# Two first blocks of expert 0 cut at different batches, with operand tiles of their own, and score banks handed over after the last scores

## The chip, the cores and the metric

The kernel runs on one core of a Trainium2 chip. A core has five engines that each work through their own instructions in order: TensorE (PE, matrix products; PEld is its weight load), VectorE (DVE), ScalarE (ACT), GpSimd (POOL) and SyncE (SP), which issues most DMA transfers. GpSimd issues the gathers and scatters by row number. Products land in PSUM, eight banks of 128 partitions by 512 fp32. The metric is the device time of one execution in microseconds (us).

## The reference

Windowed attention for 8 batches, 8 heads, 576 positions and 64 columns per head, followed by a mixture of experts over the 4608 token rows of 512 columns:

```
scores = q k^T / 8 - slope * distance, kept where 0 <= i - j < 128
attn   = softmax(scores);  x = attn v            (rows: batch, position)
noisy  = x w_gate + log(1 + exp(x w_noise)) * noise
the two best of 8 experts per row, their weights by softmax over the two
out[row] = sum over the two: weight * relu(x[row] w1[e]) w2[e]      (512 -> 1024 -> 512)
```

## The kernel before

The kernel is written out by a planner. Each piece of work is a Python generator ("strand") that asks for engines, tiles and events; `Order` keeps a simulated time, a queue by rank for every engine (lower ranks first) and rings of free tiles, and emits an instruction when the simulated engine is free. So the order on each engine is fixed when the program is built, by ranks and by constants in the head of the file (STAGE, LATE, GATE and so on), and the hardware then runs each engine's list in order. A rank is roughly a place in attention: pair k of heads and block i have 5k + i, and attention ends at 160.

**Attention.** 32 pairs of heads (4 per batch) are each cut into three units of one or two blocks of 128 queries. For a unit `unit` takes two score banks from the ring `sb` (two sets of two banks), TensorE computes scores (L493, L486), VectorE adds the bias and writes them to SBUF (`top`, L509 to L519), and gives the banks back. ScalarE takes exponentials (L526), TensorE transposes them (L533), GpSimd masks the window (L553, L554), TensorE multiplies with the values into an output bank of `ob` (L574). When the four pairs of a group are done, `row_major` turns the output into token rows: TensorE transposes, VectorE divides into a tile x (L678, a ring of four), SyncE stores it (L683) to `xs` in DRAM.

**Routing.** `gate` and `route(b)` compute the gate of a batch, choose two experts per row, count rows per expert in `base` and write every row's number into the slot lists of its experts in DRAM (a scatter on GpSimd, L900). Routing goes from batch to batch, since the counts carry over.

**Experts.** Each expert's list is worked off in blocks. `tokens` gathers a block's rows from `xs` (GpSimd, L1147), `fit` scales each row by a power of two and splits it into two fp16 parts (VectorE L1168 to L1172, ScalarE for the upper part), and a DMA transpose puts them into the operand tiles xh and xl. `ups` multiplies with a chunk of w1 into a hidden bank from `hbr` (L1200, twelve products for 128 hidden columns), `middle` takes the positive part and splits it (L1220, L1235) into hh and hl, `downs` multiplies with w2 into output banks from `yb` (L1244), and `result` scales, and scatters to `out` with an add (L1333).

**The first two blocks.** The first 768 rows of expert 0 are worked on before the lists are complete. After the routing of batch 6 (`CUT`), `base` of expert 0 is raised to at least 768 (L777), so no later row falls below, and the list's first 768 row numbers are read (`fetch_ids`, L940) and clipped to the rows of six batches (L920). Both blocks, 384 rows each, become known then. They share one pair of operand tiles xh and xl, so the second block's gathers wait until the first block's last `ups` has read them (L1228). Ranks of the two blocks go from FFN0 to FFN1, behind attention; their gathers and fits come TOKENS ranks ahead.

**Banks.** `hbr` and `yb` are empty during attention. `banks` waits until all units are done (`attended`), and hands three score banks to `hbr` and one to `yb`, then the two output banks to `yb`.

**The second wave.** When attention and routing are over, their pool of tiles is closed, a second pair of operand tiles, more weight sets and buffers are opened in its place, and the rest of expert 0 (448 rows, called the third block here) and the seven other experts follow, all on the same TensorE queue. Their weights are split to two fp16 parts on the way (L1136 for the lower part).

Of the kernel before, what the change touches and what calls it, by code (L numbers as in the profile page):

```python
# [8 lines left out]
F32 = mybir.dt.float32  # L9
F16 = mybir.dt.float16  # L10
# [11 lines left out]
NQ = 5  # L22
# [4 lines left out]
FIRST = ((0, 384), (384, 384))  # L27
FROWS = sum(c for _, c in FIRST)
# [12 lines left out]
LOAD = -26.0  # L41
VALUES = -0.5
GATE = (-11.1, 63.1)
ROUTE = 6.1
SCATTER = (9.2, -1042.6, -37.6)
FFN0, FFN1 = 178.3, 232.3
WEIGHTS = (79.4, 86.4)
TOKENS = 85.5
STAGE = (-3.5, 10.2, 17.3, -7.2, 18.8, 24.7, 17.7, -20.9)
MIDDLE = 41.7  # L50
RESULT = -82.8
# [3 lines left out]
LATE = (-6.5, -33.9, 75.9, 86.5, 26.5, -92.0, 67.3, -71.1, 43.6, -25.4, 8.5, -25.7)  # L55
# [4 lines left out]
SWITCH, NEAR = 0.093, 6.4  # L60
# [152 lines left out]
class Block:  # L213


    def __init__(self, e, s0, n, rows, rings):
        self.e, self.s0, self.n, self.rows, self.rings = e, s0, n, rows, rings
        self.last = self.flip = False
        self.tiles = [(j, min(128, n - 128 * j)) for j in range((n + 127) // 128)]
        self.ready, self.ids, self.back, self.left = Event(len(self.tiles)), Event(), Event(), len(self.tiles)  # L220
        self.weighed = Event(len(self.tiles))
        self.h = [(Event(), []) for _ in range(8)]
# [3 lines left out]
def attention_moe(ctx: ExitStack, tc: tile.TileContext, qk_, v, w_gate, w_noise, noise, w1, w2,  # L226
# [56 lines left out]
    xr = ring(ap_, 4, [128, DM], F32, "x")  # L283
# [36 lines left out]
    least = const.tile([128, 1, E], F32, name="least")  # L320
# [51 lines left out]
    def set_ups():  # L372
# [21 lines left out]
        def columns():  # L394
            reached = tmp[0:E * SPAN, 0]
            nc.vector.tensor_scalar(reached, mine, 0.0, None, op0=OP.is_ge)
            nc.vector.tensor_reduce(tmp[0:E * SPAN, 1, 0:1], reached[:, 1:E], axis=AX.X, op=OP.add)
            nc.vector.scalar_tensor_tensor(first_line, tmp[0:E * SPAN, 1, 0:1], float(LINES - SPAN), first_line,
                                           op0=OP.mult, op1=OP.add)
            nc.vector.scalar_tensor_tensor(mine, mine, float(SPAN), reached, op0=OP.is_lt, op1=OP.mult)  # L400
            nc.vector.tensor_copy(line_of[0], first_line)
            nc.vector.tensor_scalar(least[:, 0], iota8, float(NF), float(FROWS), op0=OP.is_lt, op1=OP.mult)
# [173 lines left out]
    over, attended = Event(n + B + B * NQ), Event(n)  # L576
# [10 lines left out]
    def unit(u):  # L587
# [8 lines left out]
        s = yield (sb, r0)  # L596
        yield pe((0.77, 0.98, 0.325)[gr], r0, lambda: scores(k, blocks, s), mode="rows" if nz == 2 else "full")
# [147 lines left out]
    def route(b):  # L745
# [29 lines left out]
        def up():  # L775
            if b + 1 == CUT:
                V.tensor_tensor(base, base, least[:, 0], op=OP.max)  # L777
# [131 lines left out]
        if b + 1 == CUT:  # L909
            for j in range(FROWS // 128):  # L910
                spawn(fetch_ids(j, rank))
            yield fetched
            for z in range(CUT):
                yield stored[z]

            def clipped():
                for s0, c in FIRST:
                    z = slice(s0 // 128, (s0 + c) // 128)
                    tokens_of(lists[:, z, 0], ix.bitcast(F32)[:, z], spare[:, 0:c // 128])
                nc.vector.tensor_scalar(cl, ix, float(CUT * S - 1), None, op0=OP.min)  # L920

            yield dve(0.4, rank, clipped)
            for blk in first:
                blk.ix, blk.at = (v[:, blk.s0 // 128:(blk.s0 + blk.n) // 128] for v in (ix, cl))
                mark(blk.ids)
                spawn(weights_back(blk, rank))
# [12 lines left out]
    def fetch_ids(j, rank):  # L939
        yield from move(1e4, rank, lambda: nc.sync.dma_start(lists[:, j], dram(slots, j * 128, [[1, 128], [1, 1]])))  # L940
        mark(fetched)
# [7 lines left out]
    fetched = Event(FROWS // 128)  # L949
# [21 lines left out]
    rings = {r: Ring([block_tiles(keep, r, z) for z in range(c)]) for r, c in (("xh", 1), ("xl", 1), ("hh", 3), ("hl", 3))}  # L971
    ixr, ytr = Ring([]), Ring([])
    first = [Block(0, s0, c, CUT * S, rings) for s0, c in FIRST]
# [166 lines left out]
    def tokens(blk, rank):  # L1140
        yield blk.ids
        blk.gw = yield (gwr, rank)
        blk.xh = yield (rings["xh"], rank)
        blk.xl = yield (rings["xl"], rank)
        for j, r in blk.tiles:
            xg = yield (xgr, rank)
            yield pool(1.04, rank, lambda: nc.gpsimd.indirect_dma_start(  # L1147
                out=xg[0:r], out_offset=None, in_=xs[0:blk.rows],
                in_offset=bass.IndirectOffsetOnAxis(ap=blk.at[0:r, j:j + 1], axis=0)))
            spawn(turn_tokens(blk, j, r, xg, rank))  # L1150
# [73 lines left out]
    def middle(blk, f, t, rank, end):  # L1224
        c = blk.n
        yield end
        if f == 7:
            put(rings["xh"], blk.xh)  # L1228
            put(rings["xl"], blk.xl)
# [125 lines left out]
    def banks():  # L1355

        yield attended
        scores_ = [t for two in (sb.free.pop(), sb.free.pop()) for t in two]
        for t in scores_[:3]:
            put(hbr, t)  # L1360
        put(yb, scores_[3])
# [4 lines left out]
    def second_wave():  # L1366
# [3 lines left out]
        for r in ("xh", "xl"):  # L1370
            put(rings[r], block_tiles(more, r, 1))
# [238 lines left out]
```

## Time and profile before

| what | value |
|---|---|
| median of 3 runs | 1079.54 us (1079.49 to 1082.17) |
| the profiled execution | 1074.51 us |
| its span, first to last instruction | 1072.7 us |
| busy: TensorE, VectorE, ScalarE, GpSimd | 1022.9, 703.0, 448.0, 360.1 us |
| mean granted TensorE clock | 0.991 of full speed |
| moved by DMA | 178.62 MB |

The span is that of one profiled execution; its own time is 1.8 us longer. Busy time counts an instruction from start to end, and products overlap, so a busy TensorE can still wait for short times. In a timeline row stand the start, the duration, the engine, the line, the operation, the tiles (written <- read), and in brackets the idle time before it with what ended it. A granted clock of 1.0 is 2.4 GHz, 0.5 is 1.2 GHz.

### The profile page before, as it was taken

How to read it: one execution, taken by the hardware profiler on the slowest of the kernel's cores; microseconds unless marked ns; L12 is line 12 of the kernel's file. 1: busy time of each engine (PE TensorE's matmuls, PEld its weight loads, DVE VectorE, ACT ScalarE, POOL GpSimd, SP SyncE). 2: the span in 40 equal slices, each digit the busy share in tenths (PEclk: the TensorE clock that was granted, in tenths of full speed). 3: DMA queues.
4: the chain of work that ended last, by engine and by line, in shares of the span. 5: the costliest groups of instructions: out<-in, count | busy, mean ns of one | idle time of the engine just before them, and what ended most of it. 6: DMA issues, size and time to landing. Idle time of an engine off the chain costs nothing. (4 is left out here: it accounts for less than half of the span.)

```text
span 1072.7 us, 20464 instructions
## 1 busy us (share of the span) xinstructions
PE 1022.9 (95%) x6840; PEld 600.7 (56%) x6840; DVE 703.0 (66%) x2515; ACT 448.0 (42%) x1272; POOL 360.1 (34%) x576
## 2 busy tenths in 40 slices
PE   8998999977799999999999998999999999999996
PEld 5766666654445544564456455645744574574454
DVE  8889999988664766646666567447665664673211
ACT  8977787745132332422333143314323331442211
POOL 3456656555233131222332033204222330431112
PEclk9999999989999999999999999999999999999998
DMA  8898886514295794698389676949893796776123
GB/s 324 274 311 276 292 301 209 166 49 124 57 246 132 171 223 131 159 194 207 52 185 188 170 149 112 191 136 181 122 248 63 181 191 180 137 141 84 23 34 48
DMA packets 193307, 178.62 MB, mean 167 GB/s; under 512 B 104048, under 2 KB 147344, under 8 KB 193200
## 3 DMA queue, kind: packets, MB, share of 16 engines
q1 hardware_dynamic: 175856, 138.34, 46.3%
q0 software_dynamic: 17344, 38.94, 22.4%
q8 instruction: 55, 0.90, 0.3%
q14 instruction: 52, 0.43, 0.1%
HBM read 117.29 MB, written 40.71 MB: 147 GB/s over the span
## 5 line engine op out<-in xcount | busy, mean ns | idle before, releaser
L1333 POOL DMA_INDIRECT out_dram<-yo,ix x71 | 115.8, 1631 | 509.3 <-ACT yo L265 497.9
L1235 DVE SCALAR_TENSOR_TENSOR hl<-bank,hh 128x384 f16<-128x384 f32 (+9 forms) x192 | 107.7, 562 | 249.9 <-ACT hh L1220 247.1
L1220 ACT ACTIVATE hh<-bank 128x384 f16<-128x384 f32 (+9 forms) x178 | 88.1, 495 | 439.0 <-PE bank L1200 413.5
L1244 PEld LDWEIGHTS <-hh 128*128 128x128 f16 x912 | 89.4, 98 | 97.7 <-ACT hh L1220 1.0
L1200 PE MATMUL bank<-xl,w1ha 128*128 128x384 f16 (+8 forms) x384 | 127.1, 331 | 0.5 <-DMA xl<-tl 0.5
L1200 PE MATMUL bank<-xh,w1ha 128*128 128x384 f16 (+8 forms) x384 | 127.2, 331 | 0.0
L1200 PE MATMUL bank<-xh,w1la 128*128 128x384 f16 (+8 forms) x384 | 126.9, 330 | 0.0
L1200 PE MATMUL bank<-xh,w1hb 128*128 128x512 f16 (+8 forms) x384 | 126.3, 329 | 0.0
L1200 PE MATMUL bank<-xl,w1hb 128*128 128x512 f16 (+8 forms) x384 | 126.3, 329 | 0.0
L1200 PE MATMUL bank<-xh,w1lb 128*128 128x512 f16 (+8 forms) x384 | 126.3, 329 | 0.0
L526 ACT ACTIVATE p<-p,nm 128x128 f32<-128x128 f32 x288 | 111.7, 392 | 9.6 <-DVE nm L519 9.3
L1200 PEld LDWEIGHTS <-w1ha 128*128 128x128 f16 x768 | 75.4, 98 | 55.9 <-issue 2.2
L1200 PEld LDWEIGHTS <-w1hb 128*128 128x128 f16 x768 | 74.9, 98 | 53.3
L1244 PE MATMUL bank<-w2ha,hl 128*128 128x512 f16 x228 | 87.0, 382 | 4.4 <-DVE fit L478 3.0
L1147 POOL DMA_INDIRECT xg<-xs_dram,ix x71 | 76.2, 1073 | 39.6 <-issue 14.3
L1244 PE MATMUL bank<-w2hb,hl 128*128 128x512 f16 x228 | 86.4, 379 | 0.9 <-DVE hl L1235 0.9
L1244 PE MATMUL bank<-w2ha,hh 128*128 128x512 f16 x228 | 86.7, 380 | 0.6 <-ACT hh L1220 0.6
L1244 PE MATMUL bank<-w2la,hh 128*128 128x512 f16 x228 | 86.9, 381 | 0.0
L1244 PE MATMUL bank<-w2hb,hh 128*128 128x512 f16 x228 | 86.4, 379 | 0.0
L1244 PE MATMUL bank<-w2lb,hh 128*128 128x512 f16 x228 | 86.4, 379 | 0.0
L1244 PEld LDWEIGHTS <-hl 128*128 128x128 f16 x456 | 44.9, 98 | 62.5 <-DVE hl L1235 6.5
L574 PE MATMUL bank<-pT,vraw 128*64 128x128 f32 (+2 forms) x896 | 73.5, 297 | 3.6 <-POOL pT L554 2.1
(233 smaller groups left out, 1973.4 us busy)
## 6 DMA issues: line engine op xcount, KB each, us to landing
raw<-in_w_dram SPq DMA_DIRECT2D x144, 256.0 KB
mraw<-in_w_dram SPq DMA_DIRECT2D x56, 512.0 KB
qk<-in_qk_dram SPq DMA_DIRECT2D x32, 608.0 KB
vraw<-in_v_dram SPq DMA_DIRECT2D x16, 640.0 KB
out_dram<-xg SPq DMA_DIRECT2D x10, 1024.0 KB
xs_dram<-x SPq DMA_DIRECT2D x32, 256.0 KB
xh<-th SPq DMA_TRANSPOSE x77
xl<-tl SPq DMA_TRANSPOSE x77
```

What stands on the lines that cost most here:

```text
L526: nc.scalar.activation(pv, pv, AF.Exp, bias=nm[:, z, h:h + 1], scale=-1.0, accum_out=den[:, z, 2 * g + h:2 * g + h + 1])
L574: nc.tensor.matmul(o[half, o0:o0 + c], t[:, kb, hh:hh + D], w, start=m == 0, stop=m == len(lst) - 1)
L1147: yield pool(1.04, rank, lambda: nc.gpsimd.indirect_dma_start(out=xg[0:r], out_offset=None, in_=xs[0:blk.rows], in_offset=bass.IndirectOff ...
L1200: nc.tensor.matmul(t[:, 0:blk.n], wp[:, c], x[:, c, 0:blk.n], start=c == 0 and z == 0, stop=c == 3 and z == 2)
L1220: nc.scalar.activation(o, i, AF.Relu)
L1235: yield dve(0.07 + c * 0.00104, rank - MIDDLE, lambda: nc.vector.scalar_tensor_tensor(hl[:, 0:c], t[:, 0:c], 0.0, hh[:, 0:c], op0=OP.max, ...
L1244: nc.tensor.matmul(blk.y[j][0:r], h[:, cs], wp, start=f == 0 and m == 0, stop=f == 7 and m == 2)
L1333: ins = nc.gpsimd.indirect_dma_start(out=out, out_offset=bass.IndirectOffsetOnAxis(ap=blk.ix[0:r, j:j + 1], axis=0), in_=t[0:r], in_offset ...
```

## The change

- FIRST gets a cut for each block: the first 384 rows of expert 0 are fixed after batch 3, the next 384 after batch 6 (`CUT`). `up` raises `base` twice, to 384 and to 768, and the row numbers are read, clipped and announced block by block (`first_ids`).
- Each of the two blocks has operand tiles of its own, of 384 columns (`rings1`). The shared rings start empty and get two pairs when attention's pool has been closed. The ring of x tiles goes from four to three.
- `banks` waits until every unit has been given its score banks (`asked`) and then queues for the two sets itself, so each set goes over when its last scores have been read.
- The constants that place work in the order have new values.

```diff
-FIRST = ((0, 384), (384, 384))
-FROWS = sum(c for _, c in FIRST)
+FIRST = ((0, 384, 3), (384, 384, CUT))
+FROWS = sum(c for _, c, _ in FIRST)
...
-LOAD = -26.0
+LOAD = -33.3
 VALUES = -0.5
-GATE = (-11.1, 63.1)
-ROUTE = 6.1
-SCATTER = (9.2, -1042.6, -37.6)
-FFN0, FFN1 = 178.3, 232.3
-WEIGHTS = (79.4, 86.4)
+GATE = (-11.1, 68.7)
+ROUTE = -6.5
+SCATTER = (11.6, -1040.2, -24.3)
+FFN0, FFN1 = 178.3, 224.9
+WEIGHTS = (79.4, 129.7)
 TOKENS = 85.5
-STAGE = (-3.5, 10.2, 17.3, -7.2, 18.8, 24.7, 17.7, -20.9)
-MIDDLE = 41.7
-RESULT = -82.8
+STAGE = (-0.3, 10.2, 17.3, -7.2, 11.9, 31.1, 20.2, -27.0)
+MIDDLE = 42.0
+RESULT = -65.2
...
-LATE = (-6.5, -33.9, 75.9, 86.5, 26.5, -92.0, 67.3, -71.1, 43.6, -25.4, 8.5, -25.7)
+LATE = (-6.1, -33.9, 56.9, 120.9, 26.5, -88.4, 78.2, -107.6, 47.3, 3.0, 30.5, 9.1)
...
-SWITCH, NEAR = 0.093, 6.4
+SWITCH, NEAR = 0.093, 6.9
...
-    xr = ring(ap_, 4, [128, DM], F32, "x")
+    xr = ring(ap_, 3, [128, DM], F32, "x")
...
-    over, attended = Event(n + B + B * NQ), Event(n)
+    over, attended, asked = Event(n + B + B * NQ), Event(n), Event(n)
...
         s = yield (sb, r0)
+        mark(asked)
...
         def up():
-            if b + 1 == CUT:
-                V.tensor_tensor(base, base, least[:, 0], op=OP.max)
+            for z, (*_, cut) in enumerate(FIRST):
+                if b + 1 == cut:
+                    V.tensor_tensor(base, base, least[:, z], op=OP.max)
...
-        if b + 1 == CUT:
-            for j in range(FROWS // 128):
-                spawn(fetch_ids(j, rank))
-            yield fetched
-            for z in range(CUT):
-                yield stored[z]
...
+        for blk, (s0, c, cut) in zip(first, FIRST):
+            if b + 1 == cut:
+                yield from first_ids(blk, slice(s0 // 128, (s0 + c) // 128), cut, rank)
+
+    def first_ids(blk, z, cut, rank):
+        for j in range(z.start, z.stop):
+            spawn(fetch_ids(j, rank, blk))
+        yield blk.fetched
+        for b in range(cut):
+            yield stored[b]
+
+        def clipped():
+            tokens_of(lists[:, z, 0], ix.bitcast(F32)[:, z], spare[:, 0:blk.n // 128])
+            nc.vector.tensor_scalar(cl[:, z], ix[:, z], float(cut * S - 1), None, op0=OP.min)
+
+        yield dve(0.4, rank, clipped)
+        blk.ix, blk.at = ix[:, z], cl[:, z]
+        mark(blk.ids)
+        spawn(weights_back(blk, rank))
...
-    rings = {r: Ring([block_tiles(keep, r, z) for z in range(c)]) for r, c in (("xh", 1), ("xl", 1), ("hh", 3), ("hl", 3))}
+    rings = {r: Ring([block_tiles(keep, r, z) for z in range(c)]) for r, c in (("xh", 0), ("xl", 0), ("hh", 3), ("hl", 3))}
+    rings1 = {r: Ring([keep.tile([128, 4, FIRST[z][1]], F16, name=f"{r}f{z}") for z in range(len(FIRST))]) for r in ("xh", "xl")}
...
-    first = [Block(0, s0, c, CUT * S, rings) for s0, c in FIRST]
+    first = [Block(0, s0, c, cut * S, rings1) for s0, c, cut in FIRST]
...
-        blk.xh = yield (rings["xh"], rank)
-        blk.xl = yield (rings["xl"], rank)
+        blk.xh = yield (blk.rings["xh"], rank)
+        blk.xl = yield (blk.rings["xl"], rank)
...
     def banks():
 
+        yield asked
+        for z in range(2):
+            one_, two_ = yield (sb, 0)
+            put(hbr, one_)
+            put(yb if z else hbr, two_)
         yield attended
-        scores_ = [t for two in (sb.free.pop(), sb.free.pop()) for t in two]
-        for t in scores_[:3]:
-            put(hbr, t)
-        put(yb, scores_[3])
         for _ in range(2):
             t = yield (ob, 0)
             put(yb, t)
...
         for r in ("xh", "xl"):
-            put(rings[r], block_tiles(more, r, 1))
+            for z in range(2):
+                put(rings[r], block_tiles(more, r, z))
```

## Rows read from the trace of the kernel before

**Rows 1.** The head of the profile's page: the span, and busy time, share of the span and instructions of each engine.

```profile
span 1072.7 us, 20464 instructions
...
PE 1022.9 (95%) x6840; PEld 600.7 (56%) x6840; DVE 703.0 (66%) x2515; ACT 448.0 (42%) x1272; POOL 360.1 (34%) x576
```

**Rows 2.** Busy time of each engine by stage. Columns: the stretch, its length, then busy time and number of instructions of PE, PEld, DVE, ACT and POOL, the granted clock, the DMA engines' mean busy share, GB/s.

```profile
60.00:247.00 187.00, 170.61 (x1721) 116.11 (x1717) 176.61 (x946) 139.25 (x586) 108.39 (x232) 0.98 0.67 223
247.00:264.40 17.40, 11.73 (x139) 7.39 (x136) 15.19 (x64) 7.18 (x25) 10.21 (x25) 1.00 0.55 149
264.40:307.00 42.60, 36.26 (x215) 18.69 (x212) 28.04 (x116) 6.97 (x16) 11.70 (x16) 0.92 0.49 112
...
341.60:1062.00 720.40, 714.58 (x4102) 402.15 (x4101) 412.23 (x1068) 232.44 (x409) 190.95 (x209) 1.00 0.70 145
...
1062.00:1072.70 10.70, 1.00 (x5) 0.34 (x3) 0.00 (x0) 0.68 (x1) 3.04 (x3) 0.71 0.33 45
```

**Rows 3.** Timelines of VectorE and TensorE: the last instruction on a unit's scores, and the first product of an expert.

```profile
246.80 0.08 DVE L519 DVE_READ_ACCUMULATOR2_ANT nm<- 128x1 f32 x1
...
264.42 0.48 PE L1200 MATMUL bank<-xh,w1ha 128*128 128x384 f16 x1
```

**Rows 4.** Timeline of TensorE: the first and the last of 27 second-layer products in a row, and the first and the last of 24 first-layer products in a row.

```profile
281.30 0.38 PE L1244 MATMUL bank<-w2ha,hh 128*128 128x512 f16 x1
...
286.91 0.38 PE L1244 MATMUL bank<-w2ha,hl 128*128 128x512 f16 x1
287.13 0.33 PE L1200 MATMUL bank<-xh,w1ha 128*128 128x384 f16 x1
...
290.87 0.33 PE L1200 MATMUL bank<-xh,w1la 128*128 128x384 f16 x1
```

**Rows 5.** Timeline of TensorE in the first and second block: routing's products, products after an idle time, one at the lower clock, and the first product of the third block (448 columns).

```profile
265.33 1.06 PE L675 MATMUL bank<-ident,xul 128*64 128x128 f32 x4
...
271.01 0.19 PE L769 MATMUL bank<-both,before 128*128 128x8 bf16 x2 [1.45 <-DVE both L845]
...
279.62 0.57 PE L820 MATMUL bank<-hot,hot 128*80 128x64 f16 x10 [1.12 <-DVE hot L805]
...
294.59 0.39 PE L1244 MATMUL bank<-w2ha,hl 128*128 128x512 f16 x1 [2.97 <-DVE fit L478]
...
295.43 0.63 PE L1244 MATMUL bank<-w2ha,hl 128*128 128x512 f16 x1
...
305.90 0.39 PE L1244 MATMUL bank<-w2ha,hh 128*128 128x512 f16 x1 [0.64 <-ACT hh L1220]
...
308.80 0.32 PE L1200 MATMUL bank<-xl,w1ha 128*128 128x384 f16 x1 [0.46 <-DMA xl<-tl]
...
338.76 0.35 PE L1200 MATMUL bank<-xh,w1ha 128*128 128x448 f16 x1
```

**Rows 6.** Timelines of VectorE and GpSimd for the first block's operands (row numbers clipped, first gather, first fit) and the first fit of the second block; then VectorE's instructions between 247.0 and 264.4 us by line: count, busy us, mean ns, idle us before them.

```profile
244.00 0.17 DVE L920 TENSOR_SCALAR cl<-ids 128x6 int32<-128x6 int32 x1
...
245.09 1.01 POOL L1147 DMA_INDIRECT xg<-xs_dram,cl  x1 [0.65 <-DVE x L678]
...
249.75 0.68 DVE L1168 TENSOR_REDUCE fit<-xg 128x1 f32<-128x512 f32 x1
...
291.06 0.69 DVE L1168 TENSOR_REDUCE fit<-xg 128x1 f32<-128x512 f32 x1 [7.05 <-DMA xg<-xs_dram,cl]
...
L1172 DVE SCALAR_TENSOR_TENSOR tl<-xg,fit,th 128x512 f16<-128x512 f32 x3 | 2.3, 755 | 0.0
L1168 DVE TENSOR_REDUCE fit<-xg 128x1 f32<-128x512 f32 x3 | 2.0, 679 | 0.0
...
L1163 DVE TENSOR_TENSOR gw<-xg,fit 128x1 f32<-128x1 f32 x3 | 0.7, 230 | 0.1
...
L479 DVE TENSOR_SCALAR fit<-fit 128x1 int32<-128x1 int32 x3 | 0.5, 154 | 0.1
```

**Rows 7.** Timelines of VectorE, SyncE and GpSimd in the last batch: the first and the fourth x tile written, the stores of the five, and a gather that feeds the fit at 291.06.

```profile
257.70 0.67 DVE L678 TENSOR_TENSOR x<-bank,den 128x512 f32<-128x512 f32 x1
...
262.19 0.67 DVE L678 TENSOR_TENSOR x<-bank,den 128x512 f32<-128x512 f32 x1
...
260.98 8.66 SPq L683 DMA_DIRECT2D xs_dram<-x  x5
...
287.52 1.01 POOL L1147 DMA_INDIRECT xg<-xs_dram,cl  x1 [0.30 <-issue]
```

**Rows 8.** Timelines of SyncE, VectorE and TensorE: the last transpose for the third block, and expert 1's first lower weights, written and first read.

```profile
321.38 1.20 SPq L1192 DMA_TRANSPOSE xl<-tl  x1
...
357.35 0.74 DVE L1136 SCALAR_TENSOR_TENSOR w1lb<-raw,wsc,w1hb 128x512 f16<-128x512 f32 x1
...
375.71 0.38 PE L1200 MATMUL bank<-xh,w1lb 128*128 128x512 f16 x1
```

**Rows 9.** Timelines of GpSimd and VectorE: two masks of one size, and the subtraction beside the second.

```profile
252.43 0.64 POOL L553 TENSOR_SCALAR_AFFINE_SELECT pT<-pT 128x512 f32<-128x512 f32 x1 [0.18 <-ACT pT L265]
253.14 1.12 POOL L554 TENSOR_SCALAR_AFFINE_SELECT pT<-pT 128x512 f32<-128x512 f32 x1
...
253.00 0.75 DVE L1172 SCALAR_TENSOR_TENSOR tl<-xg,fit,th 128x512 f16<-128x512 f32 x1
```

**Rows 10.** SyncE's waits from 0 to 260 us: the waiting line, whom it waited for, us in total, times, longest.

```profile
SPq L447 <- PE bank L486: 37.3, 16, 8.7
```

More of the change, by code (lines that the diff above doesn't have):

```diff
@@ L220, in __init__ @@
         self.ready, self.ids, self.back, self.left = Event(len(self.tiles)), Event(), Event(), len(self.tiles)
-        self.weighed = Event(len(self.tiles))
+        self.weighed, self.fetched = Event(len(self.tiles)), Event(len(self.tiles))
         self.h = [(Event(), []) for _ in range(8)]
@@ L319, in attention_moe @@
     base = const.tile([128, E], F32, name="base")
-    least = const.tile([128, 1, E], F32, name="least")
+    least = const.tile([128, len(FIRST), E], F32, name="least")
     rest_of_line = const.tile([128, E], F32, name="rest_of_line")
@@ L401, in columns @@
             nc.vector.tensor_copy(line_of[0], first_line)
-            nc.vector.tensor_scalar(least[:, 0], iota8, float(NF), float(FROWS), op0=OP.is_lt, op1=OP.mult)
+            for z, (s0, c, _) in enumerate(FIRST):
+                nc.vector.tensor_scalar(least[:, z], iota8, float(NF), float(s0 + c), op0=OP.is_lt, op1=OP.mult)
         yield pool(0.4, 2, small)
@@ L908, in route @@
         yield order.now + 2.5
-        if b + 1 == CUT:
-            for j in range(FROWS // 128):
-                spawn(fetch_ids(j, rank))
-            yield fetched
-            for z in range(CUT):
-                yield stored[z]
[L916 to L926, printed above, removed]
+        for blk, (s0, c, cut) in zip(first, FIRST):
[14 more added lines that the diff above has]
+        spawn(weights_back(blk, rank))
     def number_them(on, us, rank, numbered, ready):
@@ L937, in gates_out, with fetch_ids @@
         mark(sent[b])
-    def fetch_ids(j, rank):
+    def fetch_ids(j, rank, blk):
         yield from move(1e4, rank, lambda: nc.sync.dma_start(lists[:, j], dram(slots, j * 128, [[1, 128], [1, 1]])))
-        mark(fetched)
+        mark(blk.fetched)
     def tokens_of(v, t, more_rows):
@@ L946, in tokens_of @@
         nc.vector.scalar_tensor_tensor(t.bitcast(I32), v, -1.0, t, op0=OP.add, op1=OP.max)
-    fetched = Event(FROWS // 128)
     lists = keep.tile([128, FROWS // 128, 1], F32, name="list")
@@ L1227, in middle @@
         if f == 7:
-            put(rings["xh"], blk.xh)
-            put(rings["xl"], blk.xl)
+            put(blk.rings["xh"], blk.xh)
+            put(blk.rings["xl"], blk.xl)
         hh = yield (rings["hh"], rank)
```

## The prediction

> **What bounds the kernel now.** I began with the page's totals: TensorE busy 95% of a 1072.7 us span, the other engines far lower [rows 1]. A busy share averages over stages, so next came the busy time by stage. From 341.6 us to 1062 us TensorE is busy 714.58 of 720.40 us at full clock: all experts run back to back there and 5.8 us is lost in all. From 60 to 247 us, in attention, VectorE is the full engine (176.61 of 187 us) while TensorE's 170.61 us contains much pipeline latency. Between them lie two loose stretches: TensorE is busy 11.73 of 17.40 us from 247.0 to 264.4, and 36.26 of 42.60 at a mean clock of 0.92 up to 307; the last 10.7 us is the drain [rows 2]. So the end is set by when the expert products begin and by what they lose before about 340 us; after that the stream is solid.
>
> The timelines show why those stretches are loose. The last scores are read out at 246.88 us, and from then the four score banks hold nothing; the first expert product starts at 264.42 [rows 3]. Its operand is late, and so are the banks by the order of issue: rows for both blocks are numbered by the sixth batch's routing, the row numbers are clipped at 244.00, the first gather is issued at 245.09, the first fit starts at 249.75 [rows 6], and transposes follow. The second block's operands wait for the first block to give back the single pair of tiles: its fits start after 7.05 us of idle VectorE at 291.06 [rows 6], and because VectorE works in order, the first block's own product stands behind one of these fits for 2.97 us at 294.59 [rows 5].
>
> What TensorE must do from 247.0 to 338.76, where the third block's first product starts, is worked out from spacing. 27 second-layer products from 281.30 to 286.91 are 5.61 / 26 = 0.216 us apart, 24 first-layer products from 287.13 to 290.87 are 3.74 / 23 = 0.163 us apart [rows 4]. A block of 384 has 8 x 12 first and 8 x 9 second products: 96 x 0.163 + 72 x 0.216 = 15.6 + 15.5 = 31.1 us. The second block has one part of its second layer (9 x 0.216 = 1.9) beyond 338.76, so 29.2. The attention rest is 11.7. Routing in between: transposes (about 0.9, the spacing from 265.33 to the next product), one rank group (0.5) and two list groups like the one at 279.62 (0.5 each), together 2.4 [rows 5]. Sum 11.7 + 31.1 + 2.4 + 29.2 = 74.4 of 91.8 us: **17.4 us is lost**. Of it 17.40 - 11.73 = 5.7 lies before 264.4; 43.6 (264.42 to 308.01) - 31.1 - 2.4 = 10.1 lies in the first block, of which waits of 1.45, 1.12, 2.97, 0.64 and 0.46 make 6.6 [rows 5] and the remaining 3.5 is the lower clock level, 1.2 for 2.4 GHz, after an idle stretch (products of 0.63 us at 295.43 where 0.38 is full speed [rows 4, 5]); 1.6 lies in the second.
>
> **The change part by part.** *Banks.* The score banks can be used at 246.9 plus whatever attention is delayed. Three of them hold hidden units, three hidden pairs can be stored, so up to six first-layer groups (6 x 12 x 0.163 = 11.7 us) can run before any output bank is free; the output banks still wait for the last attention unit. That covers the 5.7 us. Products issued in order also stand behind attention products that are late, so I leave 2.0 of the 5.7.
>
> *Own operand tiles and cut at three.* The first block's fits no longer stand between 249.75 and 257.5, and the second block's, ready to be gathered where the first's are now, take that place. So the 2.97 us wait, the operand wait of 0.46, and both half-clock pieces (3.5) go: 6.9. What is late next are the routing waits: 1.45 and 1.12 stay, 0.64 for a hidden unit stays, the second block's 1.6 stays. Losses after: 2.0 + 1.45 + 1.12 + 0.64 + 1.6, and 0.1 left over, 6.9 in all. Won there: 17.4 - 6.9 = **10.5 us**.
>
> *What is moved into attention.* Three fits: 2.3 + 2.0 + 0.7 and four small ones of some 0.45 like L479 (1.8), 6.8 us of VectorE, and one more clip of ids, about 0.5 [rows 6]: 7.3 us. They come once the third batch is routed and ahead of later units, so before the last scores. VectorE has 187 - 176.61 = 10.4 us of idle there, in short waits [rows 2]. Bounds: 0 (all of it falls into waits) and 7.3 (none does). I take two thirds, 4.9, nearer to the full engine. The 3 scaled copies on ScalarE (139.25 of 187 busy) and the 3 gathers on GpSimd (108.39) cost nothing under that cover; uncovered they cost at most 3 x 0.7 and 3 x 1.0 us. The six transposes, some 7.4 us of SyncE's queue, go ahead of later query and key loads; these already wait 37.3 us in total for a tile to come free [rows 10], with four tiles in use, so I count 0; one tile late would show as TensorE waiting for the load.
>
> The fit's subtraction reads two SBUF operands. Beside one that starts at 253.00 the mask on GpSimd took 1.12 us, where a neighbour of the same size took 0.64 [rows 9]. The Trainium skill ("SBUF — State Buffer", section on SBUF's two separate sides) says that VectorE with two SBUF inputs and a GpSimd instruction that reads SBUF exclude each other for a whole instruction. By that rule three subtractions could hold masks up by 2.3 us and the sum would be 2.3 us worse; by the row it is about 0.5 each, on an engine with 40% to spare, and nothing.
>
> *Three output staging tiles (x) for four.* In the last batch the fourth tile is written at 262.19 while the first one's store is issued at 260.98, behind the transposes on SyncE [rows 7]. A gather issued at 287.52 feeds a fit at 291.06, after 1.0 of issue some 2.5 us of transfer; so that store lands near 260.98 + 0.3 + 2.5 = 263.8, and VectorE would wait 1.6 us. It falls on the last batch's routing, which has slack (below): 0 in the sum, up to 3.2 (two such waits) in the range.
>
> *What is late afterwards.* The third block's operands need the last batch: their last transpose is issued at 321.38, and they are wanted at 338.76. That transpose stood behind the second block's six tiles of work, gone from there, so it comes no later even if attention ends 4.9 later. Expert 1's first residual weights are done at 357.35 + 0.74 and read at 375.71 [rows 8]: 17.6 us of slack. Reordered priorities in the solid stage: its 5.8 us of loss can shrink or grow by one stall of about 3 us; I count 0.
>
> *Sum.* 4.9 - 10.5 = **-5.6 us**. The profiled run took 1074.51 us (1.8 outside its span), so its counterpart is 1068.9. The median of the runs shown is 1079.54, 5.0 above it with the same code; the difference is carried over: **1073.9 us**.
>
> **The rivals.** (A) *VectorE eats it.* All 7.3 us of moved work delays the scores, and the 10.1 us in the first block stays, because the routing chain on VectorE still holds the hidden units back. Then only 5.7 - 2.0 = 3.7 is won: +3.6, or 1083.1; with the 2.97 wait gone, +0.6, or 1080.2, which I take. For it: VectorE 94% busy. Against: the rows name a fit, not routing, for the largest wait.
> (B) *It is hidden better.* The moved fits fall wholly into waits and the filler takes the whole 5.7 and half of the routing waits: 17.4 - 3.6 = -13.8, or 1065.7. For it: 10.4 us of idle VectorE. Against: these are short waits in an engine that works in order.
> (C) *The three x tiles stall VectorE in attention: slower.* Each wait of 1.6 us is paid in full by the units behind. If all eight batches bunch their tiles like the last one, 8 x 1.6 = 12.8; -5.6 + 12.8 = +7.2, or 1086.7. It decides from four batches on (6.4 > 5.6), and it passes 0.3% from six. For it: the bunch at 257.70 to 262.19. Against: most stores are issued within a microsecond when SyncE is not held by transposes.
> That the change does nothing is no rival: the third batch holds enough rows for 384 of expert 0, so no slot is padded (416 of them with the inputs drawn from seed 0).
>
> **How the numbers follow.** Forecast 0.51, A 0.19, B 0.13, C 0.17. A measurement of this kernel tells about 0.3% (3.2 us) from no change. Faster: 0.51 with a tenth off for falling within 3.2, B, and a little of A: 0.61. Same: most of A and that tenth: 0.20. Slower: C and a rest of A: 0.19. The range reaches from B with 2 us of the solid stage (1064) to 1082.5, past A and short of C; the forecast's own, with 0 to 7.3 for the moved work and 3 either way later, is 1068 to 1079.
>
> **What would show it.** Right: the first expert product within 3 us of the last score read; three fits and six transposes of the first block before the scores end; no wait of a second-layer product for a fit; the last scores read 3 to 7 us later than 246.9; the third block's first product near 333. Wrong: the last scores read more than 8 us later, waits on x stores, TensorE waiting for query and key loads, or a third block that waits for its operands.

## The result: 0.7% slower, and the profile after

The changed kernel takes 1087.12 us (median of 20 runs, 1083.74 to 1091.04), the kernel before 1079.51 (20 runs, 1073.24 to 1084.88). The ratio is 1.0071, 95% interval 1.0054 to 1.0089: 7.6 us slower, where 5.6 us faster was forecast. 1087.1 is nearly the number of rival C, but C's mechanism is not in the trace.

The page's head after, which answers to [rows 1]:

```profile
span 1088.1 us, 20477 instructions
PE 1028.4 (95%) x6840; PEld 604.4 (56%) x6840; DVE 703.8 (65%) x2519; ACT 446.5 (41%) x1271; POOL 361.1 (33%) x576
```

Busy time by stage, columns as in [rows 2]: attention to the last score read, from there to the third block's first product, and the rest.

```profile
60.00:271.10 211.10, 179.30 (x1715) 120.62 (x1715) 178.56 (x965) 143.17 (x593) 113.53 (x239) 0.92 0.65 206
271.10:353.60 82.50, 75.12 (x512) 41.45 (x513) 54.56 (x207) 20.86 (x51) 28.54 (x47) 0.98 0.54 144
353.60:1078.00 724.40, 718.67 (x4120) 403.56 (x4117) 420.66 (x1075) 228.85 (x404) 190.40 (x209) 1.00 0.70 145
```

Read the first row beside [rows 2]. VectorE's work hardly grew (178.56 for 176.61 us), but the stretch is 24 us longer, so the engine that had been full is now idle for 32 us, and the mean granted clock is 0.92. Time was not filled with moved work; something stands still. The second row, 82.5 us, answers to 91.9 us before (246.88 to 338.76). So behind the scores some 9 us were won, where 10.5 had been forecast, and in attention more than that was lost.

VectorE's waits and GpSimd's say where. First the timeline of GpSimd in the changed kernel, three pieces (L903 is the scatter of slot numbers, L1151 a gather of the first block, L648 a copy in `sums`):

```profile
97.51 1.67 POOL L903 DMA_INDIRECT slots_dram<-listed,line_of  x1 [0.19 <-DVE nm L520]
104.67 0.18 POOL L648 COPY den<-den 64x4 f32<-64x4 f32 x1 [5.48 <-DMA slots_dram<-listed,line_of]
...
164.26 1.52 POOL L903 DMA_INDIRECT slots_dram<-listed,line_of  x1 [0.57 <-DVE den L652]
172.81 0.18 POOL L648 COPY den<-den 64x4 f32<-64x4 f32 x1 [7.03 <-DMA slots_dram<-listed,line_of]
...
203.29 1.03 POOL L1151 DMA_INDIRECT xg<-xs_dram,cl  x1 [0.15 <-issue]
...
211.24 0.18 POOL L648 COPY den<-den 64x4 f32<-64x4 f32 x1 [5.12 <-DMA xg<-xs_dram,cl]
```

A copy of 0.18 us, which moves four columns of sums from partitions 64-127 to 0-63, waits 5.48, 7.03 and 5.12 us, 17.6 us in all, for a scatter or for gathers, though it reads nothing that they write. VectorE stands behind it in the same three places, its reciprocal of the sums being next in its list:

```profile
105.21 0.19 DVE L652 RECIPROCAL den<-den 64x8 f32<-64x8 f32 x1 [2.13 <-POOL den L649]
...
173.35 0.20 DVE L652 RECIPROCAL den<-den 64x8 f32<-64x8 f32 x1 [7.42 <-POOL den L649]
...
211.78 0.20 DVE L652 RECIPROCAL den<-den 64x8 f32<-64x8 f32 x1 [5.62 <-POOL den L649]
...
271.00 0.08 DVE L520 DVE_READ_ACCUMULATOR2_ANT nm<- 128x1 f32 x1
```

The last row answers to [rows 3]: the last scores are read 24.2 us later. TensorE, which needs the masks of GpSimd or the scores that VectorE reads, shows the same three places, then the first expert product and the third block's:

```profile
105.95 2.38 PE L575 MATMUL bank<-pT,vraw 128*64 128x64 f32 x16 [3.46 <-POOL pT L555]
...
174.74 1.01 PE L487 MATMUL bank<-qk 128*128 128x192 f32 x2 [6.83 <-DVE nm L520]
...
213.18 0.69 PE L713 MATMUL bank<-ident,gt 128*128 128x128 f32 x2 [5.64 <-DVE x L680]
...
269.75 0.32 PE L1204 MATMUL bank<-xhf,w1ha 128*128 128x384 f16 x1 [0.46 <-DVE nm L520]
...
332.47 0.39 PE L1248 MATMUL bank<-w2ha,hl 128*128 128x512 f16 x1 [1.37 <-DVE fit L479]
...
353.66 0.35 PE L1204 MATMUL bank<-xh,w1ha 128*128 128x448 f16 x1
```

In the kernel before no such copy stood so close behind a transfer. Its GpSimd timeline at the first of the three places:

```profile
93.71 0.18 POOL L646 COPY den<-den 64x4 f32<-64x4 f32 x1
...
94.87 1.65 POOL L900 DMA_INDIRECT slots_dram<-listed,line_of  x1 [0.51 <-PE bank L574]
```

There the copy comes ahead of the scatter by a few instructions. In the changed kernel it comes right behind, at the second place too (in the kernel before the copy is at 162.08 us and the scatter at 165.06), and at the third place behind the gathers that were moved into attention. In the list of GpSimd's instructions as built, with the semaphores that each waits for, the changed kernel has at the first place:

```
134 L903 DMA slots_dram<-listed,line_of 704x64   [waits DMAHW2, DVE]
135 L648 COPY den<-den 64x4                      [waits DMASW0, Pool]
136 L649 TENSOR_SCALAR den<-den 64x8             [waits Pool]
```

DMASW are the transfers that GpSimd itself has issued. The wait is written into the program, and the planner, which knows only 0.4 us for these two instructions, does not know of it. The built list of the kernel before has such waits too, at each copy that comes behind a new transfer; there the transfer has landed when the copy's turn comes.

### The profile page after: what moved, and what is told of

Its sections match the earlier page's. It is cut to its first block, busy times and chain, and to the rows that moved or that the text cites. A ratio compares the mean times of both kernels' runs of the same rounds, so it can differ in the third digit from the quotient of the medians.

```text
span 1088.1 us, 20477 instructions
## 1 busy us (share of the span) xinstructions
PE 1028.4 (95%) x6840; PEld 604.4 (56%) x6840; DVE 703.8 (65%) x2519; ACT 446.5 (41%) x1271; POOL 361.1 (33%) x576
## 5 line engine op out<-in xcount | busy, mean ns | idle before, releaser
L527 ACT ACTIVATE p<-p,nm 128x128 f32<-128x128 f32 x288 | 111.6, 393 | 13.4 <-DVE nm L520 13.0
L1204 PE MATMUL bank<-xh,w1la 128*128 128x384 f16 (+8 forms) x320 | 105.4, 329 | 0.0
L1204 PE MATMUL bank<-xh,w1ha 128*128 128x384 f16 (+8 forms) x320 | 105.4, 329 | 0.0
L1204 PE MATMUL bank<-xl,w1ha 128*128 128x384 f16 (+8 forms) x320 | 105.4, 329 | 0.0
L1151 POOL DMA_INDIRECT xg<-xs_dram,ix x71 | 77.8, 1095 | 36.8 <-issue 15.8
L575 PE MATMUL bank<-pT,vraw 128*64 128x128 f32 (+2 forms) x896 | 75.9, 305 | 9.5 <-POOL pT L555 9.3
```

Source lines behind the costliest of these rows:

```text
L527: nc.scalar.activation(pv, pv, AF.Exp, bias=nm[:, z, h:h + 1], scale=-1.0, accum_out=den[:, z, 2 * g + h:2 * g + h + 1])
L575: nc.tensor.matmul(o[half, o0:o0 + c], t[:, kb, hh:hh + D], w, start=m == 0, stop=m == len(lst) - 1)
L1204: nc.tensor.matmul(t[:, 0:blk.n], wp[:, c], x[:, c, 0:blk.n], start=c == 0 and z == 0, stop=c == 3 and z == 2)
```

## The experiments

T1: the copies' waits for GpSimd's own transfers are the loss. T2: VectorE is full and pays for the moved fits (rival A). T3: three x tiles hold VectorE up (rival C). T4: the new constants themselves.

### The copy taken off GpSimd: e1 and e2

```diff
         def sums():
-            if nz == 1:
-                nc.gpsimd.tensor_copy(den[0:64, 0, 1:H:2], den[64:128, 0, 0:H:2])
             nc.gpsimd.tensor_scalar(den[0:nr, 0:nz], den[0:nr, 0:nz], 1e-9, None, op0=OP.add)
...
+        def soft_():
+            soft(g, blocks, p, nm, den)
+            softs[b, gr] = softs.get((b, gr), 0) + 1
+            if nz == 1 and softs[b, gr] == NP:
+                nc.scalar.activation(den[0:64, 0, 1:H:2], den[64:128, 0, 0:H:2], AF.Copy)
```

e1 is the changed kernel with this edit. In the two built lists TensorE, VectorE and SyncE have the same instructions in the same order; eight copies move from GpSimd to ScalarE, and nothing else.

> The changed kernel with one edit: the small copy of sums from partitions 64-127 to 0-63 (one per batch, 64x4 values), which stands in GpSimd's list and there waits for every transfer that GpSimd has issued, is done by ScalarE right behind the exponentials that wrote the sums. Eight instructions move; nothing else changes place on any engine. Theory T1 (the loss is these copies: placed right behind a scatter at 104.67 and 172.81 us and behind three gathers at 211.24 us they held GpSimd 5.48 + 7.03 + 5.12 = 17.6 us, VectorE behind them 15.2 us): the three idles are gone, the last scores are read at 247 to 253 us instead of 268.4, and the time is 15 to 24 us shorter, 1063 to 1072 us, ratio to the kernel before 0.985 to 0.993. Theory T2 (VectorE is full and pays for the fits moved into attention) and T3 (three x tiles hold VectorE up): the waits on GpSimd only stand in for time that VectorE lacks anyway; last scores at 264 to 268 us, ratio 1.003 to 1.009.

Measured: 1072.58 us, ratio 0.9926 (0.9899 to 0.9952). (The 268.4 us that the expectation gives for the changed kernel's last scores is wrong; they are read at 271.08.) e1's GpSimd at the first two places:

```profile
97.87 1.66 POOL L907 DMA_INDIRECT slots_dram<-listed,line_of  x1 [0.19 <-DVE nm L520]
99.60 0.24 POOL L653 TENSOR_SCALAR den<-den 64x8 f32<-64x8 f32 x1
...
158.71 1.50 POOL L907 DMA_INDIRECT slots_dram<-listed,line_of  x1 [0.57 <-DVE den L656]
160.28 0.23 POOL L653 TENSOR_SCALAR den<-den 64x8 f32<-64x8 f32 x1
```

The idles are gone, and ScalarE's eight copies cost 1.6 us of that engine in all. The last scores are read at 251.17 us. Busy time around the second place, first the changed kernel, then e1:

```profile
160.00:180.00 20.00, 13.17 (x109) 8.76 (x108) 11.49 (x77) 11.14 (x48) 8.95 (x21) 0.83 0.54 169
```

```profile
160.00:180.00 20.00, 19.99 (x210) 13.42 (x208) 19.48 (x111) 16.45 (x69) 10.37 (x25) 1.00 0.91 290
```

In 20 us TensorE has 109 instructions in the one and 210 in the other: the stall stops the whole pipeline. The clock granted behind it falls from 2.4 towards 1.2 GHz: 0.55 from 106 to 116 us, 0.63 from 172 to 176 and 0.50 from 213 to 221, behind the three idles, where it had been 1.00 from 60 to 97. So 17.6 us of idle GpSimd became 19.9 us later scores; what the clock has in this was not measured by itself. T2 and T3 had 1.003 to 1.009 for e1 and are out as causes of the loss.

e2 is the kernel before with the same edit.

> The kernel before with the same edit: the eight copies are done by ScalarE. T1: in the kernel before each copy stands long behind the last scatter in GpSimd's list, so no wait goes away; ratio 0.997 to 1.003, last scores at 246 to 248 us. A rival (the copy on GpSimd is dear wherever it stands): ratio below 0.995.

Measured: 0.9996 (0.9969 to 1.0023). The copy itself costs nothing where it stands well behind a transfer.

### What waits, the data or the way across partitions: e5 and e6

Both add one instruction to e1, at the old places: `nc.gpsimd.tensor_copy(other2[0:64], X)`, where X is `other[64:128]` in e5 and `other[0:64]` in e6, tiles that nobody else uses.

> The kernel of e1 (copies of the sums on ScalarE) with a small GpSimd copy of an unrelated, constant tile at the eight old places, from partitions 64-127 to 0-63 like the one removed. Its result is read by nothing. T1 in the sharper form T1s (what waits for GpSimd's outstanding transfers is any GpSimd copy from one half of the partitions to the other, whatever its data): the three idles of 5 to 7 us are back at the same places, last scores at 264 to 273 us, time 12 to 20 us above e1's, ratio 1.004 to 1.010. Rival T1d (the wait came from the data, the sums that other engines read): no idle, ratio as e1, 0.990 to 0.995.

> As e5, but the dummy copy stays in its partitions (0-63 to 0-63). T1s: no idle at the copies, ratio as e1, 0.990 to 0.995, last scores at 249 to 253 us. Rival T1c (any copy on GpSimd behind a transfer waits): as e5, 1.004 to 1.010.

Measured: e5 1.0063 (1.0039 to 1.0088), the changed kernel's time again; e6 0.9889 (0.9850 to 0.9928), e1's time within the intervals. The waits of GpSimd from 60 to 272 us in e5 (who, for what, us in total, times, longest):

```profile
POOL other L656 <- DMA slots_dram<-listed,line_of: 12.8, 2, 7.3
POOL other L656 <- DMA xg<-xs_dram,cl: 4.2, 1, 4.2
```

And e6's timeline, the level copy behind the same scatter:

```profile
97.59 1.67 POOL L911 DMA_INDIRECT slots_dram<-listed,line_of  x1 [0.19 <-DVE nm L522]
98.76 0.71 POOL L656 COPY other<-other 64x4 f32<-64x4 f32 x1
99.54 0.24 POOL L657 TENSOR_SCALAR den<-den 64x8 f32<-64x8 f32 x1
```

A dummy copy across the halves brings the three idles, 17.0 us, and the whole loss back; the same copy within its partitions starts before the scatter's own span is over. The built lists differ in this alone: e5's copies wait for DMASW semaphores, e6's for none. So T1s stands: as these programs are built, a GpSimd copy from one half of the partitions to the other waits until the transfers GpSimd has issued before it have landed, whatever its data. Whether the chip needs that wait was not tried, since no wait was taken away by itself.

### Constants and structure apart: e3, e4, e10, e11

e3 is the kernel before with the new constants, e4 the change with the old ones; e11 and e10 are the same two with the copies on ScalarE.

> The kernel before with the changed kernel's constants (LOAD to SWITCH, all values of the diff) and none of its structure. In its GpSimd list one copy (batch 2's) stands directly behind a scatter, the other seven stand 12 or more instructions behind one. T1: one idle of 5 to 7 us in front of that copy, last scores about 7 us later than before (252 to 256 us), ratio 1.003 to 1.010. Theory T4 (the new constants themselves cost what the change costs): the whole 24 us in attention, ratio 1.007 or more with no idle at a copy.

> The changed kernel's structure with the constants of the kernel before. In its GpSimd list batch 2's copy stands directly behind a scatter and batch 5's copy six instructions behind the second of three gathers. T1: two idles of 4 to 7 us, last scores at 254 to 264 us, time between the kernel before less 5 and plus 5 us, ratio 0.995 to 1.005. T2: one fit's worth of work more on VectorE is paid whether or not there is an idle at a copy: last scores 5 to 8 us late, ratio 0.995 to 1.001. T4: the old constants bring the loss back to nothing, ratio below 0.995.

> The kernel of e4 (structure of the change, constants of before) with the copies on ScalarE. e4 showed one idle of 5.81 us at a copy and ratio 1.0025. T1: the idle goes, 5 to 9 us with it, ratio 0.993 to 0.998. Theory T4 in its weak form (constants and structure only fit together): the loss stays, ratio above 1.000.

> The kernel of e3 (structure of before, constants of the change) with the copies on ScalarE. e3 had one idle of 6.35 us at a copy, but took 25 us more than before, far above T1's 1.003 to 1.010. T1 for its share: 5 to 9 us go with the idle, ratio 1.014 to 1.019; the rest is the order that constants found for two pairs of tiles give with one pair. If the copy's wait is the whole of it: 0.998 to 1.004. If it has no part in it: 1.021 to 1.026.

| kernel | structure | constants | copies on | ratio, 95% interval |
|---|---|---|---|---|
| e3 | before | new | GpSimd | 1.0235 (1.0208 to 1.0262) |
| e11 | before | new | ScalarE | 1.0142 (1.0099 to 1.0184) |
| e4 | changed | old | GpSimd | 1.0025 (0.9999 to 1.0051) |
| e10 | changed | old | ScalarE | 0.9994 (0.9964 to 1.0023) |
| e1 | changed | new | ScalarE | 0.9926 (0.9899 to 0.9952) |

e3 missed its expectation: the one idle is there,

```profile
95.00 1.65 POOL L900 DMA_INDIRECT slots_dram<-listed,line_of  x1 [0.65 <-DVE nm L519]
103.00 0.18 POOL L646 COPY den<-den 64x4 f32<-64x4 f32 x1 [6.35 <-DMA slots_dram<-listed,line_of]
```

but it is 0.9% of the 2.35% (the ratios of e3 and e11, some 10 us). The rest is not one thing. Beside e2, the kernel before with its copies on ScalarE, e11 reads its last scores 6.2 us later (254.11 for 247.95) and comes to expert 1 14.9 us later (394.72 for 379.87). Behind the scores e3's TensorE waits 5.23 us for a transpose of the shared operand tiles at 316.84 us and 6.92 us for a hidden unit at 331.11. Constants found for two pairs of tiles don't suit one pair, and old ones don't suit two: e10 wins nothing.

e4 had two idles, of 5.81 us at the first place and 2.13 at another (240.77 us); batch 5's copy, for which the expectation had the second, came 4.6 us behind the gather's start and did not wait. Without these 7.9 us e10's last scores come only 1.3 us earlier (262.25 for 263.50), and its ratio lies between T1's range and T4's, with an interval that touches e4's. So an idle of GpSimd is not paid in full in every order; what it costs in the changed kernel's order is shown by e1 and e5, 1.4 to 1.5% of the time. At the first place either one alone, structure or constants, turns the copy behind the scatter (e3, e4). T4 is thus a part of the picture, but not of the sign: with the copies on ScalarE the new constants win.

### The parts of the change: e7, e8, e9, e13 to e16

All are edits of e1, but e16 of e2. e7: `ring(ap_, 4, [128, DM], F32, "x")`. e8: the old `banks()`. e9: `FIRST = ((0, 384, CUT), (384, 384, CUT))`. e13 and e14 repeat e1 and e8 side by side on one chip; e15 has the edits of e8 and e9 together; e16 adds the new `banks()` to e2.

> The kernel of e1 with four x tiles instead of three; the order changes where the planner meets the ring. T3 in small (the forecast's rival C): each batch pays up to 1.6 us for the third tile, so the last scores are read up to 12.8 us earlier than e1's 251.1 us and the time falls by 3 to 12 us, ratio below 0.990. T1: the ring costs nothing measurable; ratio 0.989 to 0.996, last scores at 249 to 253 us.

> The kernel of e1 with the old hand-over of the banks: all score banks go over only when the last unit has left attention. The forecast booked 3.7 us (5.7 less 2.0 left over) for the new hand-over. If that holds: first expert product 10 us or more behind the last score read instead of 1.3 us ahead, third block's first product 3 to 5 us later than e1's 332.7, ratio 0.995 to 0.998. Rival (the tiles of its own alone give the whole gain, since the banks' time is filled later anyway): third block's first product within 1 us of e1's, ratio 0.991 to 0.994.

> The kernel of e1 with both first blocks cut after batch 6 again (new banks, own operand tiles, new constants stay; copies on ScalarE). The forecast put 4.9 us of moved fits against the 6.9 us won by own tiles and the early cut together. If the early cut is what wins: the first block's operands come as late as in the kernel before, first expert product at 258 to 266 us, last scores at 246 to 249 us (nothing is moved ahead), ratio 0.995 to 1.000. Rival (own tiles alone give the gain, the cut only moves work forward): third block's first product within 2 us of e1's 332.7, ratio 0.989 to 0.994.

> The kernel of e1 again, on one chip with e14 to e16, so that the parts are compared side by side. Expected as e1 and e6: ratio 0.989 to 0.994.

> The kernel of e8 (e1 with the old hand-over of banks) beside e13. Up to the end of attention TensorE's order is that of e13. If the new hand-over costs time: 2 us or more below e13, ratio 0.984 to 0.988. If it is worth nothing either way, because the third block's first product stands at 332.7 and 332.9 us with and without it: within 2 us of e13. If it wins 3.7 us as forecast: 3 to 4 us above e13.

> The change's own operand tiles, three x tiles and constants, with both blocks cut after batch 6, the old hand-over of banks, and the copies on ScalarE: cut and hand-over undone together. Forecast's ledger: the hand-over's 3.7 us and most of the cut's gain are gone, ratio 0.997 to 1.002. Rival (as e8 and e9 suggest, the parts do not add up; what TensorE wins before the third block is given back behind it): ratio 0.988 to 0.995.

> The kernel of e2 (before, copies on ScalarE) with the new hand-over of banks alone. The first block's row numbers still come with batch 6, at 244 us, so its first product cannot start before its first operands at about 262 us. Forecast's ledger: up to 3.7 us won, ratio 0.996 to 0.998. Rival (banks were not what the first product waited for; its operands were): within 1 us, ratio 0.997 to 1.003, first expert product at 262 to 266 us.

Four points of each profiled run in us, read from the timelines (end of the last score read, first products of the first block, of the third block and of expert 1), beside the ratio of the timed runs:

| kernel | scores | first | third | expert 1 | ratio, 95% interval |
|---|---|---|---|---|---|
| before | 246.88 | 264.42 | 338.76 | 375.27 | 1 |
| e2, before, copies moved | 247.95 | 265.86 | 342.86 | 379.87 | 0.9996 (0.9969 to 1.0023) |
| e16, new banks alone | 246.65 | 264.70 | 344.33 | 380.84 | 1.0005 (0.9982 to 1.0027) |
| e15, own tiles alone | 246.24 | 266.21 | 337.48 | 373.99 | 0.9917 (0.9895 to 0.9939) |
| e9, tiles and banks | 245.99 | 266.31 | 338.72 | 375.24 | 0.9927 (0.9904 to 0.9951) |
| e8, tiles and early cut | 253.03 | 262.17 | 332.90 | 371.36 | 0.9858 (0.9826 to 0.9891) |
| e14, as e8 | 253.33 | 263.80 | 333.96 | 372.44 | 0.9875 (0.9852 to 0.9898) |
| e1, all three | 251.17 | 249.83 | 332.71 | 374.35 | 0.9926 (0.9899 to 0.9952) |
| e13, as e1 | 251.45 | 250.11 | 333.09 | 373.00 | 0.9901 (0.9872 to 0.9931) |
| changed, copies on GpSimd | 271.08 | 269.75 | 353.66 | 392.18 | 1.0071 (1.0054 to 1.0089) |

The first row needs care: it is an execution 5.0 us faster than its kernel's median. e2 and e16, whose timed runs equal the kernel before, come to expert 1 at 379.87 and 380.84 us. So a few us between two single executions say little, and the ratios decide.

Own tiles, with the constants that go with them, carry most of the gain: e15 alone has 0.8%. With the new hand-over of banks the early cut adds nothing to it: it costs some 5 us of attention (e9 to e1: 245.99 to 251.17) and brings the third block 6.0 us forward, but at expert 1 only 0.9 us is left, and no difference in the timed runs. With the old hand-over it does add: e14 takes 1067.62 us and e15 beside it 1072.02, 0.4% less, with intervals that just touch, and e8 0.6% less on another chip. The new hand-over starts expert products 12 us earlier (249.83 for 262.17) and wins nothing: the third block starts at the same time, and beside each other e14 is 3.8 us below e13 in medians, with intervals that overlap, so a loss is likely and not settled. Alone, in e16, it does nothing: the last transpose for the first block is issued at 258.63 us there, and the first product stands at 264.70. e8 lies below both of its expectations, and e9 meets its rival's in the ratio, but not in the third block's start.

What holds TensorE there is seen in e1's timeline, the second block's last stretch and the third block's begin:

```profile
311.18 0.39 PE L1252 MATMUL bank<-w2ha,hh 128*128 128x512 f16 x1 [2.48 <-ACT hh L1228]
...
313.15 0.52 PE L1252 MATMUL bank<-w2ha,hl 128*128 128x512 f16 x1 [1.37 <-DVE fit L479]
...
332.71 0.35 PE L1208 MATMUL bank<-xh,w1ha 128*128 128x448 f16 x1
...
337.14 0.61 PE L1252 MATMUL bank<-w2ha,hl 128*128 128x512 f16 x1 [3.26 <-DVE fit L479]
```

and in its GpSimd, VectorE and ScalarE: the last slot scatter, the first fit of the third block and the scaled copy behind it, and a fit of expert 1's first block:

```profile
291.47 1.43 POOL L907 DMA_INDIRECT slots_dram<-listed,line_of  x1 [2.13 <-issue]
...
308.74 0.69 DVE L1176 TENSOR_REDUCE fit<-xg 128x1 f32<-128x512 f32 x1 [6.71 <-DMA xg<-xs_dram,ix]
...
310.03 0.72 ACT L265 ACTIVATE th<-xg,fit 128x512 f16<-128x512 f32 x1 [8.59 <-DVE fit L1168]
...
335.27 0.69 DVE L1176 TENSOR_REDUCE fit<-xg 128x1 f32<-128x512 f32 x1 [2.14 <-DMA xg<-xs_dram,ix]
```

VectorE stands 6.71 us in order before a fit of the third block, ScalarE 8.59 us for its result, and the hidden units of the second block stand behind both. That fit hangs on the last batch's routing, whose scatter is issued at 291.47 us with the new banks and at 291.39 without (e8). TensorE's waits there are about as long without the new hand-over: 3.98 us in e8 and 4.54 in e14, for 4.5 in e1 and 4.1 in e13. The wait at 337.14 is another: there the second block's last products stand behind fits of expert 1's first block. e13 has it too, with 2.82 us, and e8 and e14 don't: from the third block's first product to expert 1's they take 38.5 us, e1 and e13 41.6 and 39.9.

e7 fits neither expectation: 0.9994 (0.9970 to 1.0017), the last scores at 263.79 us, 12.6 later than with three tiles and with no idle at a copy. With one more tile the planner lays another order: e7's TensorE list departs from e1's at its 206th instruction, and VectorE has 189.5 us of work from 60 us to the last score, where e1 has 179.7. For rival C it suffices that no kernel here has VectorE waiting for a store of x; the tile's price by itself can't be read from e7.

### A try at the third block's queue: e12

A block's gathers are issued one behind the other (e8's kernel, `join=False` for the gather), so that the third block's four stand ahead of the result scatters.

> The kernel of e8 (old hand-over of banks, copies on ScalarE) in which a block's gathers are issued one behind the other, so that the third block's four gathers stand ahead of the first block's three result scatters on GpSimd; in e8 they alternate, a gather issued at 299.25 us is used at 305.94, and TensorE waits 3.98 us at 315.00 for a fit behind them. If that queue is what holds the third block: this wait falls below 1.5 us, the third block's first product comes 2 to 4 us earlier than 332.9, ratio 0.982 to 0.985. Rival (VectorE's order, not the gathers, holds it): the same waits elsewhere, ratio 0.985 to 0.990.

Measured: 0.9960 (0.9934 to 0.9987), slower than e8 and outside both expectations. The edit changed attention's order too: the last scores came at 261.14 us instead of 253.03, third block at 340.18, and TensorE still waited 4.06 us at 337.22, now for a hidden unit. Whether the queue holds the third block stays open.

The best version is e8 and e14, the change with its copies on ScalarE and the old hand-over: 1068.11 and 1067.62 us, 1.4% and 1.25% below the kernel before.

## Why the prediction was wrong, point by point

**The step that failed** is "What is moved into attention", and it failed twice. First in one clause: "The 3 scaled copies on ScalarE (139.25 of 187 busy) and the 3 gathers on GpSimd (108.39) cost nothing under that cover; uncovered they cost at most 3 x 0.7 and 3 x 1.0 us". It priced the gathers by how busy GpSimd is and by their issue time. The price is what stands behind them: a copy across partitions that waits until they land, 5.12 us at the third place. Second, the sum looked for new priorities only "in the solid stage". In attention it put the new order at nothing, and that order, by structure or constants, has slot scatters directly ahead of two such copies, 5.48 and 7.03 us. GpSimd's bound of 3.0 us met 17.6 us of idle and 19.9 us of later scores (271.08 against e1's 251.17). The size could have been bounded: [rows 6] shows a gather's issue at 245.09 and its fit at 249.75, so an instruction that waits for it pays some 4.7 us. The question was who on GpSimd waits for a transfer at all, and the copy did not show it in the trace before, since there it always came late enough.

**What held.** The rest of the ledger is measured by e1, which is the change without that wait:
- Moved work, 4.9 us of bounds 0 to 7.3: the last scores are 4.3 us later than before. This holds for e1's order alone; in e10 and e7, other orders of the same work and with no idle at a copy, they are 15.4 and 16.9 us later.
- From the last score to the third block's first product, 10.5 us to win: 91.9 to 81.5 us, 10.3 won; third block forecast "near 333", measured 332.71. So close an agreement is partly luck: e2, which times like the kernel before, takes 94.9 us there, and beside it 13.4 are won.
- Sum -5.6 us, or 0.9948; measured 0.9926 and 0.9901, that is 8.0 and 10.7 us. The sign and the order of size are right; e1's interval holds the forecast, e13's does not.
- By the Trainium skill ("SBUF — State Buffer", section on SBUF's two separate sides) a mask and such a subtraction exclude each other, and the prediction named 2.3 us for this beside its sum. In e1 no mask ran beside the first block's three subtractions (193.46, 200.28 and 204.64 us), and from 60 us to the last score GpSimd's masks took 66.3 us, before 66.6. One small GpSimd sum beside the second subtraction took 0.55 us, where e13's, with none beside it, took 0.21. So no run here shows what the rule would have cost.

**What held in sum but not in its parts.** 3.7 us of the 10.5 were booked to the banks. e8 and e16 find nothing of it. Own tiles give 0.8%, and the early cut adds to them only with the old hand-over. "I count 0" for the third block's operands was wrong in the small: its fits hold the second block's products (2.48 and 1.37 us in e1, 3.98 in e8). Nor did the sum count the wait for expert 1's fits, 3.26 us in e1.

**The rivals.** A (VectorE eats it): VectorE was idler than before in the changed kernel, and without the copies' waits attention paid 4.3 us, not 7.3. B (all hidden in waits): the scores were later in e1 too. C gave the right number, 1086.7, by luck: no trace shows its mechanism. None of them had GpSimd as the bound.

**The signs named.** The alarm "last scores more than 8 us later" rang, with 24.2 us. The first expert product came 1.3 us before the end of the last score read, and the first block's six transposes ran from 213.57 to 228.28 us, within attention, as written. "No wait of a second-layer product for a fit" was wrong in the changed kernel and in e1, with the third block's and expert 1's fits in place of the second's. "Near 333" came true in e1 and not in the changed kernel, where the third block starts at 353.66 us.

## What to carry to other kernels

An engine's idle share does not price an instruction put into its queue: look at what stands behind it, and in the built list at which semaphores that waits for. A wait that never shows because its transfer has always landed is still there, and a new order alone, without a new instruction, can bring it out (e3). Where a planner lays the order, give it such waits as costs, or take them away, as ScalarE's 0.2 us copies did here; and when an edit lets it reshuffle (e7, e12: last scores 8 to 13 us later), read the time against the order before the edit is blamed.

## What was not expected of the hardware

A GpSimd copy between the halves of the partitions, 0.18 us long, stood 4.20 to 7.28 us for a scatter or gather that GpSimd had issued (e5), the same copy within its half did not (e6). This is a wait that the built program holds; whether the hardware needs it is open. ScalarE read partitions 64-127 and wrote 0-63 in 0.205 us, with no such wait. e1's eight of them in the page's groups (count, busy us, mean ns, idle before):

```profile
L616 ACT ACTIVATE den<-den 64x4 f32<-64x4 f32 x8 | 1.6, 205 | 0.3
```

The slot scatter issued at 97.51 us held the copy until 104.67: some 7 us, as the waiting copy sees it, for a transfer whose issue takes 1.67.
